# Three early query and key loads in the raw words' ring, a later third sequence, and block (0, 2) ahead of group 1

## The chip, the core and the metric

The kernel runs on one core of one Trainium2 chip. The metric is the device time of one execution in microseconds (us); three runs of the kernel before gave 728.9, 729.03 and 730.33, median 729.03.

## The reference

Three layers follow one another, all in float32.

```python
def _attn_ref(q, k, v):                      # (4, 8, 576, 64)
    scores = scale * np.matmul(q, k.transpose(0, 1, 3, 2))
    mask_local = (rel >= 0) & (rel < stride)             # heads 0 to 3, stride 32
    mask_strided = (rel >= 0) & (pos[None, :] % stride == pos[:, None] % stride)   # heads 4 to 7
    ...
    return np.matmul(attn, v)                # softmax of the masked scores times v

def _moe_ref(x, w_in, w_out, s, b):          # x (2304, 512), w_in (512, 2048), w_out (2048, 512)
    r = np.maximum(x @ w_in, 0.0)
    return (s * (r * r) + b) @ w_out

def _moe2_ref(x, w_gate, w1, w2):            # 8 experts, 288 tokens each, routed by the order of the logits
    ...
        h = np.maximum(x[mask] @ w1[e], 0.0)
        out[mask] = h @ w2[e]
```

The inputs of the second layer come as float64 words ("raw words"); the kernel makes float32 of them on the chip.

## The kernel before

**Stages.** `run` calls `mix1`, which holds the attention and the first product of the second layer; then come the second product with the routing, and the eight experts. Only `mix1` is touched. A matmul in full precision is three matmuls: every operand is split into a high part (`xh`, `wh`, `u`) and the rest (`xl`, `wl`).

**Attention.** Four sequences b of 576 tokens. `attention` yields its units, a head pair hp and a half hf each: `attn_pair` for the strided pairs, `attn_unit` for the local ones. A unit loads queries and keys (`load_unit`, L222: a tile `qk`), makes scores on PE (L264 mask, L271 products), takes the maximum on DVE (L289, L390), the exponential on ACT (L314, L395), scales on DVE, transposes on PE (L329, L420), copies to `eT` on ACT (L335, L432), multiplies with v on PE (L341, L443), and copies to `xb` on ACT (L363, L448). For the sequences 2 and 3 the mask is added on DVE instead (L307). Two pipes tick through the units: `att` for the sequences 0 and 1, `att2` for 2 and 3. `LOADLAG`, `lag` and the `yield`s say how many ticks lie between the steps of a unit.

**Words.** `prep` turns the raw words of `w_in` into `win[fc]`, fc = 0 to 15: load (L514), ACT L539, four DVE operations (L542 to L548), then `split` (ACT L524 for `wh`, DVE L526 for `wl`).

**Groups.** The tokens are cut into six groups g of 384. `group_x` (L480) splits a group's columns into `xh` (ACT L493) and `xl` (DVE L496). `h_step(g, fc)` (L633) is one block: twelve matmuls of 384 columns on PE (L641; xh times wh, xl times wh, xh times wl), two ACT operations (L653, L654), and a store to `ud` (L657). In what follows h(g, fc) is such a block.

**Order.** The program's order is each engine's order: the schedule is written by hand (`manual_schedule`). A first loop of `mix1` counts k and ticks `att`, from k = `A2K` on also `att2`, until 14 units are done; at k = 33 and 37 (`H0`) it issues h(0, 0) and h(0, 1), at k = 34 eight matmuls that only keep PE busy (L469). A second loop then walks through `seq`: after the first two blocks (1, 0), (1, 1), (0, 2), (1, 2), (0, 3), (1, 3), (2, 0), (2, 1) and so on, one block for each pass, with a tick of the pipes ahead of it. The subtractions of group 0 are collected in `self.subs` and issued at k = 30 (`XL`); those of later groups at once.

**Rings.** A tile comes from a ring of buffers, and a load into it waits until what used the buffer before is through. `qk` has the ring "u" of four (`UB`), so the load of unit n waits for the scores of unit n - 4. `wide` has the ring "rw" of four (`RW`), which before the experts holds the raw words of `w_in` alone. PE's results go to eight banks (`ps`). All loads of this stage are issued by SP, in order; a load that waits holds back those behind it.

Of the kernel before, what the change touches and what calls it, by code (L numbers as in the profile page):

```python
# [8 lines left out]
F32 = mybir.dt.float32  # L9
# [20 lines left out]
def _f(ap):  # L30
    return ap.bitcast(F32)
# [14 lines left out]
class Pipe:  # L46


    def __init__(self, items, every=1):
        self.items, self.every, self.t, self.live, self.started = iter(items), every, 0, [], 0  # L50
# [27 lines left out]
class Body:  # L78
# [21 lines left out]
    FP = 9  # L100
    FC = 8
    UB = 4
    WL = 64
    P1S = 31
    A2K = 35
    TM = 2
    FE = (12, 12, 4, 8)
    PS = (18, 30, 32, 36)
# [29 lines left out]
    def __init__(self, ctx, tc, a, dbg=()):  # L138
        self.tc, self.nc, self.a, self.dbg = tc, tc.nc, a, dbg
        self.c = ctx.enter_context(tc.tile_pool(name="c", bufs=1))  # L140
        self.w = ctx.enter_context(tc.tile_pool(name="w", bufs=self.WS))
        self.xf = ctx.enter_context(tc.tile_pool(name="xf", bufs=2))
        self.xs = ctx.enter_context(tc.tile_pool(name="xs", bufs=self.XS))
        self.p2 = ctx.enter_context(tc.tile_pool(name="p2", bufs=2))
        self.pp = ctx.enter_context(tc.tile_pool(name="pp", bufs=8, space=bass.MemoryType.PSUM))
        self.dr = ctx.enter_context(tc.tile_pool(name="dr", bufs=1, space=bass.MemoryType.DRAM))
        self.n = 0

    def nm(self, s):
        self.n += 1  # L150
# [71 lines left out]
    def load_unit(self, b, hp, hf):  # L222
        nc, a = self.nc, self.a
        loc = hp < 2
        w = 320 if loc and not hf else 288
        qk = self.p2.tile([128, 640], F32, tag="u", name=self.nm("qk"), bufs=self.UB)[:, :2 * w]
        if loc and not hf:
            src = a["q0"][b, hp]
        else:
            src = a["q1"][b, hp // 2 * (1 + hf), hp % 2]  # L230
        nc.sync.dma_start(qk, src.rearrange("p a t -> p (a t)"))
        return qk.rearrange("p (a t) -> p a t", a=2)
# [247 lines left out]
    def group_x(self, g, dc):  # L480
        nc = self.nc
        S, G = self.S, self.G
        if g == 2:
            h, l = (self.wt([128, G], F32R, n) for n in ("xh", "xl"))
        else:
            h, l = (self.xs.tile([128, G], F32R, tag=n, name=self.nm(n)) for n in ("xh", "xl"))
        t = g * G
        while t < (g + 1) * G:
            b = t // S
            e = min((b + 1) * S, (g + 1) * G)  # L490
            src = self.xb[b][:, dc, t - b * S:e - b * S]
            o = slice(t - g * G, e - g * G)
            nc.scalar.copy(h[:, o], src)  # L493

            def sub(l=l[:, o], h=h[:, o], src=src):
                nc.vector.tensor_tensor(l, src, _f(h), op=ALU.subtract)  # L496

            if g:
                sub()
            else:  # L500
                self.subs.append(sub)
            t = e
        self.xg.setdefault(g, {})[dc] = h, l
# [233 lines left out]
    def mix1(self):  # L737
# [24 lines left out]
        self.late = self.x2_late()  # L762
        self.late_pipe = Pipe(self.late_step(g, fc) for g in range(self.NG) for fc in range(16))
        lead = len(self.H0)
        seq = [(0, fc) for fc in range(lead)] + [(1, 0), (1, 1), (0, 2), (1, 2), (0, 3), (1, 3), (2, 0), (2, 1)]
        for fc in range(2, 14):
            seq += [(0, fc + 2), (2, fc), (1, fc + 2)]
        seq = [s for s in seq if s[1] < 16 - self.TAIL * (s[0] > 0)]
# [7 lines left out]
        while self.units < 14 or not self.win or ready:  # L776
            rest, self.rest = self.rest, []
            if k in self.H0:
                assert len(self.xg[0]) == 4 and not self.subs
                main.tick()  # L780
            self.attend(att, att2 if k >= self.A2K else None, mid=first.tick if k == self.P1A else None)
            for part in rest:
# [20 lines left out]
        while True:  # L803
            g, fc = seq[n] if n < 96 else (n // 16, n % 16)
            k += 1
            if n == 4:
                self.small_loads()
            if n >= self.P1S:
                prep1.tick()
            if len(self.win) < 16:  # L810
                prep.tick()
                if len(self.win) <= fc:
                    continue
            if n == 10:
                att2.every = self.AE
            self.attend(att, att2)
            while ready and self.units >= ready[0][0]:
                self.group_x(*ready.pop(0)[1:])
            if g == 2 and ready:
                continue  # L820
            if n >= self.FS:
                for _ in range(self.FT):
                    if folds.started < len(order) and order[folds.started][1] >= self.nwog:
                        break
                    folds.tick()
            if n >= self.WL and (n % 2 == 0 or n >= 84) and (lout.started < self.nwog or lout.started == 16):
                lout.tick()
            if n >= 95 and self.late_pipe.t < 6:
                self.late_pipe.tick()
            if n == 44 or fc == 12 and 2 < g < 5:  # L830
                need = 8 * (((n // 16 + 2) * self.G - 1) // self.S + 1)
                while self.units < need:
                    self.attend(att2)
            if n == self.RC:
                self.route_consts()
            if n >= 96:
                for _ in range(self.LF):
                    next(self.late, None)
            live = main.tick()
            if 44 <= n < 48 or fc >= 12 and 2 < g < 5:  # L840
                self.group_x(n // 16 + 1, n % 16 - 12)
            n += 1
            if not live and not folds.live and folds.started == len(order) and lout.started == 16 and not lout.live:
                break

    def late_step(self, g, fc):
# [7 lines left out]
        if last:  # L854
            u = self.p2.tile([128, 2, 320], F32R, tag="u", name=self.nm("u"), bufs=self.UB)[:, :, :nt * 128]
            u = u[:, 0], u[:, 1]
# [324 lines left out]
    def expert(self, e, X, w1, w2):  # L1181
# [3 lines left out]
        def step(fc):  # L1185
            ps = self.layer1(fc, X, w1)
            yield
            u = self.p2.tile([128, 2, 320], F32R, tag="u", name=self.nm("u2"), bufs=self.UB)
            self.relu_split(ps, u[:, 0, :288], u[:, 1, :288])
# [192 lines left out]
```

## Time and profile before

| | |
|---|---|
| median of three runs | 729.03 us (728.9 to 730.33) |
| profiled execution, its own time | 732.19 us |
| its span, first to last instruction | 730.1 us |
| PE busy with matmuls | 717.0 us, 98% of the span |
| PEld (weight loads), DVE, ACT | 643.2, 490.8, 382.6 us |
| DMA queue q1 | 129.68 MB |

The profiled execution took 732.19 us, 2.1 more than its span, and 3.2 more than the median of the runs without a profile. A row of a list in order of time has the start, the length, the engine, the line, the operation with what it writes and reads, the count, and in brackets the idle time ahead of it with what ended that. "issue" is idle time in which the engine waited for nothing that the profile shows.

### The profile page before, as it was taken

How to read it: one execution, taken by the hardware profiler on the slowest of the kernel's cores; microseconds unless marked ns; L12 is line 12 of the kernel's file. 1: busy time of each engine (PE TensorE's matmuls, PEld its weight loads, DVE VectorE, ACT ScalarE, POOL GpSimd, SP SyncE). 2: the span in 40 equal slices, each digit the busy share in tenths (PEclk: the TensorE clock that was granted, in tenths of full speed). 3: DMA queues.
4: the chain of work that ended last, by engine and by line, in shares of the span. 5: the costliest groups of instructions: out<-in, count | busy, mean ns of one | idle time of the engine just before them, and what ended most of it. 6: DMA issues, size and time to landing. Idle time of an engine off the chain costs nothing. (4 is left out here: it accounts for less than half of the span.)

```text
span 730.1 us, 16583 instructions
## 1 busy us (share of the span) xinstructions
PE 717.0 (98%) x6298; PEld 643.2 (88%) x6298; DVE 490.8 (67%) x1151; ACT 382.6 (52%) x876; POOL 58.6 (8%) x80
## 2 busy tenths in 40 slices
PE   8999999999999999999999999999999999999996
PEld 6779999999999888787888878888999999999995
DVE  6899798895653344286888888784566667667720
ACT  4788676777776565522432423241554655555521
POOL 3000000000000000000000000001212321322111
PEclk9999999999999999999999999999999999999999
DMA  8857786666988779733553424252867666765411
GB/s 235 255 164 213 234 258 197 222 204 220 317 292 274 225 250 321 251 127 121 183 163 127 160 82 132 94 163 74 275 196 234 213 177 210 238 206 158 151 33 32
DMA packets 82350, 140.16 MB, mean 192 GB/s; under 512 B 10592, under 2 KB 44128, under 8 KB 82272
## 3 DMA queue, kind: packets, MB, share of 16 engines
q1 hardware_dynamic: 79200, 129.68, 55.6%
q0 software_dynamic: 3072, 9.44, 4.2%
q8 instruction: 49, 0.80, 0.5%
q14 instruction: 29, 0.24, 0.1%
HBM read 106.32 MB, written 32.77 MB: 190 GB/s over the span
## 5 line engine op out<-in xcount | busy, mean ns | idle before, releaser
L897 PE MATMUL b<-wh,u 128*128 128x512 f32 x612 | 173.6, 388 | 0.3 <-DVE u L869 0.3
L897 PEld LDWEIGHTS b<-wh,u 128*128 128x128 f32 x612 | 110.6, 190 | 14.5 <-DVE u L869 1.3
L1197 PE MATMUL b<-u,wh 128*128 128x288 f32 x496 | 88.8, 292 | 0.0
L866 ACT CAST u<-r 128x384 fp32r<-128x384 f32 (+1 forms) x96 | 46.0, 493 | 79.2 <-DMA r<-ud 30.9
L641 PE MATMUL b<-xh,wh 128*128 128x384 f32 x384 | 83.6, 340 | 1.3 <-DVE E L307 1.2
L1172 PE MATMUL b<-X,wh 128*128 128x288 f32 x512 | 84.1, 287 | 0.1
L524 ACT CAST wh<-raw 128x512 fp32r<-128x512 f32 x128 | 73.2, 617 | 11.7 <-DVE u L869 11.7
L641 PE MATMUL b<-xh,wl 128*128 128x384 f32 x384 | 78.2, 326 | 0.0
L641 PE MATMUL b<-xl,wh 128*128 128x384 f32 x384 | 78.1, 326 | 0.0
L897 PE MATMUL b<-wl,u 128*128 128x512 f32 x204 | 77.6, 380 | 0.0
L653 ACT ACTIVATE r<-b 128x384 f32<-128x384 f32 x96 | 46.9, 489 | 57.0 <-PE b L641 51.9
L526 DVE TENSOR_TENSOR wl<-raw,wh 128x512 fp32r<-128x512 f32 x112 | 73.0, 684 | 0.4
L1197 PEld LDWEIGHTS b<-u,wh 128*128 128x128 f32 x496 | 72.9, 189 | 0.0
L1172 PEld LDWEIGHTS b<-X,wh 128*128 128x128 f32 x512 | 71.7, 189 | 1.0 <-ACT X L1139 0.3
L641 PEld LDWEIGHTS b<-xh,wh 128*128 128x128 f32 x384 | 61.8, 189 | 7.7 <-PE b L685 1.9
L641 PEld LDWEIGHTS b<-xh,wl 128*128 128x128 f32 x384 | 64.9, 189 | 0.1
L641 PEld LDWEIGHTS b<-xl,wh 128*128 128x128 f32 x384 | 64.9, 189 | 0.0
L1179 DVE SCALAR_TENSOR_TENSOR u<-b,u 128x288 fp32r<-128x288 f32 x64 | 29.1, 455 | 49.6 <-ACT u L1178 47.0
L869 DVE TENSOR_TENSOR u<-r,u 128x384 fp32r<-128x384 f32 (+1 forms) x96 | 47.8, 528 | 10.0 <-ACT u L866 10.0
L654 ACT ACTIVATE r<-r 128x384 f32<-128x384 f32 x96 | 50.5, 526 | 3.0
L1178 ACT ACTIVATE u<-b 128x288 fp32r<-128x288 f32 x64 | 26.3, 411 | 47.3 <-PE b L1172 44.9
L1197 PE MATMUL b<-u,wl 128*128 128x288 f32 x176 | 50.3, 286 | 0.0
(234 smaller groups left out, 1118.7 us busy)
## 6 DMA issues: line engine op xcount, KB each, us to landing
raw<-in_moe_w_dram SPq DMA_DIRECT2D x128, 256.0 KB
r<-ud SPq DMA_DIRECT2D x160, 192.0 KB
ud<-r SPq DMA_DIRECT2D x96, 192.0 KB
raw<-in_words_dram SPq DMA_DIRECT2D x16, 512.0 KB
raw<-in_words_dram SPq DMA_DIRECT2D x32, 256.0 KB
qk<-in_q_dram SPq DMA_DIRECT2D x24, 288.0 KB
x2d<-E SPq DMA_DIRECT2D x18, 256.0 KB
wod<-K SPq DMA_DIRECT2D x16, 256.0 KB
```

The lines of the kernel that those rows point to most:

```text
L524: nc.scalar.copy(h, W)
L526: nc.vector.tensor_tensor(l, W, _f(h), op=ALU.subtract)
L641: nc.tensor.matmul(ps[:, :self.G], w[:, dc * 128:(dc + 1) * 128], _alt(self.xg[g][dc][x]), start=(w is wh and x == dc == 0), stop=(w is wl ...
L653: nc.scalar.activation(_two(r), _nat(ps[:, :self.G]), AF.Relu)
L654: nc.scalar.activation(r, r, AF.Square)
L866: nc.scalar.copy(d[0], src)
L869: nc.vector.tensor_tensor(d[1], src, _f(d[0]), op=ALU.subtract)
L897: self.nc.tensor.matmul(**args)
L1172: self.nc.tensor.matmul(ps[:, :288], w1[dc, fh][wi][:, fs:fs + 128], _alt(X[:, xi, dc, :]), start=(k == 0), stop=(k == 11))
L1178: self.nc.scalar.activation(_two(h), _nat(ps[:, :288]), AF.Relu)
L1179: self.nc.vector.scalar_tensor_tensor(_two(l), _nat(ps[:, :288]), 0.0, _two(_f(h)), op0=ALU.max, op1=ALU.subtract)
L1197: nc.tensor.matmul(y[dc][:, :288], w[:, sl], _alt(u[:, j, :288]), start=(fc == 0 and i == 0), stop=(fc == 7 and i == 2))
```

## The change

Four edits. `WQ` names the 6th, 10th and 14th load of queries and keys (counted from 0: 5, 9, 13); these take a buffer of the ring "rw" instead of one of "u". `A2K` goes from 35 to 38, so that `att2` begins three passes later. In `seq`, (0, 2) stands ahead of (1, 0) and (1, 1). The subtraction for the last columns of group 1, `group_x(1, 1)`, is collected in `self.subs`, and the second loop issues what is collected there ahead of its tick of the pipes.

```diff
+    WQ = (5, 9, 13)
...
-    A2K = 35
+    A2K = 38
...
-        self.n = 0
+        self.n = self.nq = 0
...
-        qk = self.p2.tile([128, 640], F32, tag="u", name=self.nm("qk"), bufs=self.UB)[:, :2 * w]
+        if self.nq in self.WQ:
+            qk = self.wide([128, 1024], F32, "qk")
+        else:
+            qk = self.p2.tile([128, 640], F32, tag="u", name=self.nm("qk"), bufs=self.UB)
+        self.nq += 1
+        qk = qk[:, :2 * w]
...
-            if g:
+            if g and (g, dc) != (1, 1):
                 sub()
             else:
                 self.subs.append(sub)
...
-        seq = [(0, fc) for fc in range(lead)] + [(1, 0), (1, 1), (0, 2), (1, 2), (0, 3), (1, 3), (2, 0), (2, 1)]
+        seq = [(0, fc) for fc in range(lead)] + [(0, 2), (1, 0), (1, 1), (1, 2), (0, 3), (1, 3), (2, 0), (2, 1)]
...
                 if len(self.win) <= fc:
                     continue
+            for sub in self.subs:
+                sub()
+            self.subs.clear()
             if n == 10:
                 att2.every = self.AE
```

SP, about 13 to 20 us into the span, before (`qk` are queries and keys, `v` values, `raw` raw words; in brackets what the load waits for, PE being the scores that free its buffer):

```order
L231 DMA qk_470<-in_q_dram 128x576 [waits DMAHW4_49,PE_49]
L243 DMA v_480<-in_v_dram 96x512 [waits DMAHW5_49]
L231 DMA qk_500<-in_q_dram 128x576 [waits DMAHW6_49,PE_49]
L514 DMA raw_520<-in_words_dram 128x1024 [waits DMAHW7_49]
L243 DMA v_540<-in_v_dram 96x512 [waits DMAHW0_49]
L231 DMA qk_592<-in_q_dram 128x640 [waits DMAHW1_49,PE_49]
L231 DMA qk_635<-in_q_dram 128x576 [waits DMAHW2_49,PE_49]
```

The same place in the changed kernel:

```order
L237 DMA qk_470<-in_q_dram 128x576 [waits DMAHW4_49,PE_49]
L249 DMA v_480<-in_v_dram 96x512 [waits DMAHW5_49]
L237 DMA qk_500<-in_q_dram 128x576 [waits DMAHW6_49]
L520 DMA raw_520<-in_words_dram 128x1024 [waits DMAHW7_49]
L249 DMA v_540<-in_v_dram 96x512 [waits DMAHW0_49]
L237 DMA qk_592<-in_q_dram 128x640 [waits DMAHW1_49,PE_49]
L237 DMA qk_635<-in_q_dram 128x576 [waits DMAHW2_49,PE_49]
```

No load has moved; the tenth, qk_500, has lost its wait for PE, and the others wait for scores that are one to three units older.

PE, about 51 to 56 us, where group 1 begins, before (b are PE's banks; xh_956 is of group 1, wh_700 of win[0], qk_1111 of sequence 2):

```order
L443 MATMUL b_1130<-eT_1099,v_945 64x64 x2
L641 MATMUL b_1154<-xh_956,wh_700 128x384
L641 MATMUL b_1154<-xh_1119,wh_700 128x384
L641 MATMUL b_1154<-xh_883,wh_700 128x384
L641 MATMUL b_1154<-xh_1080,wh_700 128x384
L641 MATMUL b_1154<-xl_957,wh_700 128x384
L641 MATMUL b_1154<-xl_1120,wh_700 128x384
```

The same place in the changed kernel (xh_760 and xl_761 are of group 0, wh_1088 of win[2], qk_1082 of sequence 2):

```order
L449 MATMUL b_1109<-eT_1079,v_945 64x64 x2
L277 MATMUL b_1122<-qk_1082 36x36 x16
L647 MATMUL b_1150<-xh_760,wh_1088 128x384
L647 MATMUL b_1150<-xh_763,wh_1088 128x384
L647 MATMUL b_1150<-xh_766,wh_1088 128x384
L647 MATMUL b_1150<-xh_769,wh_1088 128x384
L647 MATMUL b_1150<-xl_761,wh_1088 128x384
```

The first scores of sequence 2 stand here now, and no longer in the middle of h(0, 1); h(0, 2) follows them in the place of h(1, 0).

DVE, about 51 to 55 us, before:

```order
L496 TENSOR_TENSOR xl_1081<-xb_369,xh_1080 128x192
L496 TENSOR_TENSOR xl_1081<-xb_872,xh_1080 128x192
L307 TENSOR_TENSOR E_103<-b_1057,mstr 36x8x36 x2
L496 TENSOR_TENSOR xl_1120<-xb_369,xh_1119 128x192
L496 TENSOR_TENSOR xl_1120<-xb_872,xh_1119 128x192
L526 TENSOR_TENSOR wl_1108<-K_983,wh_1107 128x512
```

And in the changed kernel:

```order
L502 TENSOR_TENSOR xl_1061<-xb_369,xh_1060 128x192
L502 TENSOR_TENSOR xl_1061<-xb_872,xh_1060 128x192
L532 TENSOR_TENSOR wl_1089<-K_983,wh_1088 128x512
L502 TENSOR_TENSOR xl_1099<-xb_369,xh_1098 128x192
L502 TENSOR_TENSOR xl_1099<-xb_872,xh_1098 128x192
```

The two mask additions of sequence 2 have left this place, and `wl` of win[2] goes ahead of the subtraction of `group_x(1, 1)`.

## Rows read from the trace of the kernel before

**Rows 1.** The page: busy time; DMA queues (packets, MB, share); issues (count, KB)

```profile
PE 717.0 (98%) x6298; PEld 643.2 (88%) x6298; DVE 490.8 (67%) x1151; ACT 382.6 (52%) x876; POOL 58.6 (8%) x80
...
q8 instruction: 49, 0.80, 0.5%
...
raw<-in_words_dram SPq DMA_DIRECT2D x16, 512.0 KB
```

**Rows 2.** What PE waited for, whole span: us in total, times, longest

```profile
PE b L264 <- DVE identb L189: 3.2, 1, 3.2
PE b L271 <- issue: 1.5, 1, 1.5
PE b L641 <- DVE E L307: 1.2, 1, 1.2
PE b L897 <- DVE u L869: 0.3, 1, 0.3
```

**Rows 3.** Busy time of each engine by stretch, granted clock (PEclk), DMA share

```profile
16.00:20.00 4.00, 4.00 (x92) 3.24 (x91) 3.67 (x10) 3.21 (x17) 0.00 (x0) 1.00 0.71 191
21.20:24.50 3.30, 3.27 (x131) 2.78 (x131) 2.52 (x7) 3.30 (x15) 0.00 (x0) 1.00 1.03 291
...
28.00:31.40 3.40, 3.40 (x40) 2.78 (x36) 3.15 (x7) 1.32 (x6) 0.00 (x0) 0.50 0.90 288
...
60.00:100.00 40.00, 40.00 (x424) 37.73 (x424) 34.97 (x63) 28.44 (x58) 0.00 (x0) 1.00 0.79 250
```

**Rows 4.** PE in order of time, around the early stall

```profile
15.03 1.04 PE L271 MATMUL b<-qk 64*64 64x96 f32 x20
...
23.79 0.68 PE L271 MATMUL b<-qk 64*36 64x36 f32 x28
25.97 0.26 PE L271 MATMUL b<-qk 64*36 64x36 f32 x4 [1.50 <-issue]
...
27.78 1.73 PE L271 MATMUL b<-qk 64*64 64x96 f32 x20
```

**Rows 5.** DMA queues from 23.0 to 23.5 us: packets, MB, share

```profile
q8 instruction: 1, 0.02, 16.2%
```

**Rows 6.** Who waited for whom, 0 to 75 us: SP's loads, PE's weight loads

```profile
PEld b L271 <- DMA qk<-in_q_dram: 0.4, 2, 0.3
...
SPq L231 <- PE b L271: 8.3, 8, 1.9
```

**Rows 7.** PE in order of time, from h(0, 1) to h(0, 3)

```profile
46.35 0.92 PE L641 MATMUL b<-xh,wh 128*128 128x384 f32 x4
47.10 0.81 PE L641 MATMUL b<-xl,wh 128*128 128x384 f32 x4
47.84 0.75 PE L271 MATMUL b<-qk 64*36 64x36 f32 x32
48.53 0.75 PE L420 MATMUL b<-identf,E 128*96 128x128 f32 x4
49.21 0.80 PE L443 MATMUL b<-eT,v 96*64 96x64 f32 x20
49.94 0.92 PE L641 MATMUL b<-xh,wl 128*128 128x384 f32 x4
50.69 0.60 PE L420 MATMUL b<-identf,E 128*96 128x128 f32 x4
51.22 0.69 PE L443 MATMUL b<-eT,v 96*64 96x64 f32 x16
53.15 0.92 PE L641 MATMUL b<-xh,wh 128*128 128x384 f32 x4 [1.24 <-DVE E L307]
...
62.74 0.81 PE L641 MATMUL b<-xh,wh 128*128 128x384 f32 x4
```

**Rows 8.** ACT in order of time, the same stretch

```profile
48.23 0.72 ACT L432 COPY eT<-b 96x384 f32<-96x384 f32 x2
...
50.33 0.66 ACT L432 COPY eT<-b 96x256 f32<-96x256 f32 x2
51.75 0.62 ACT L524 CAST wh<-K 128x512 fp32r<-128x512 f32 x1 [0.77 <-DVE K L548]
```

**Rows 9.** DVE in order of time, the same stretch

```profile
52.18 0.92 DVE L307 TENSOR_TENSOR E<-b,mstr 36x288 f32<-36x288 f32 x2
...
61.32 0.69 DVE L526 TENSOR_TENSOR wl<-K,wh 128x512 fp32r<-128x512 f32 x1
```

## The prediction

> **What bounds the kernel now.** I read the page's busy times first: PE is busy for 717.0 us of a span of 730.1, 98%, more than any other engine [rows 1]. So an edit is worth what it takes off PE's idle time or adds to it, and anything else only if it makes PE's own work longer. Next I read what PE waited for. There are three waits of more than a microsecond: 3.2 us at the start, for a constant; 1.5 us ahead of scores, for nothing that the profile shows ("issue"); and 1.2 us ahead of a block, for DVE's L307 [rows 2]. The table by stretch shows a fourth loss: from 28.0 to 31.4 us the granted clock is 0.50, that is 1.2 GHz and not 2.4 [rows 3]. Behind 53 us PE has no idle time worth a row until the second product; from 60 to 100 us it is busy for 40.00 of 40.00 us [rows 3]. The four edits all act ahead of about 150 us, so they can win at most the second and third wait and the slow stretch. What they can lose is a new wait.
>
> **The change part by part. Removed: the wait at 51.9 us.** PE's h(1, 0) starts at 53.15 after 1.24 us of idle time, which DVE's L307 ended [rows 7]. L307 is the mask addition of sequence 2 and runs from 52.18 to 53.10 [rows 9]; it reads a bank that PE wants back. With A2K at 38 the scores that L307 reads are made later, and L307 leaves this place in DVE's order; h(0, 2), which now comes first, needs group 0, long split, and win[2]. So that wait goes. What is late next is found by replaying PE from 46.35 with the durations of the rows, start to start. The first eight matmuls of h(0, 1) end at 47.84. The scores that stood there (0.69 us) are gone, so the transposes run from 47.84 to 48.52 (0.68). The products behind them want eT, which ACT finishes at 48.23 + 0.72 = 48.95 [rows 8]: a new wait of 0.43. They take 0.73, the last four matmuls of h(0, 1) take 0.75, the transposes 0.53 [rows 7]: 50.96. The next products want eT at 50.33 + 0.66 = 50.99 [rows 8]: 0.03 of waiting. They take 0.69: 51.68. The first scores of sequence 2, moved here, take 0.69: 52.37. The wh of win[2] is ready at 51.75 + 0.62 = 52.37 [rows 8]. So h(0, 2) starts at 52.37 with the same work behind it as h(1, 0) had at 53.15: **0.78 us won**. Of the 1.24 us, 0.46 come back as waits for eT, because the moved scores had covered ACT. Bounds: nothing, if some other operand binds at 53.1; the whole 1.24 if ACT, too, runs ahead.
>
> **Moved: blocks, subtraction, sequence 2.** The order of the blocks costs nothing on PE, since the same twelve matmuls are issued; what counts is that operands are there. The wl of win[2] is the next DVE operation behind wh: 52.37 + 0.69 = 53.06, and the last four matmuls of h(0, 2) want it 1.5 us after 52.37 (46.35 to 47.84, [rows 7]), at 53.86. The deferred subtraction of group_x(1, 1) stands behind that, 0.63 us long, done by about 53.7; h(1, 0) starts two microseconds after 52.37, and wants it later still. Win[3], for h(0, 3), gains: DVE's wl for it ends at 61.32 + 0.69 in the kernel before, behind a mask addition, a maximum and a subtraction of sequence 2, and these now come later; PE starts h(0, 3) at 62.74 [rows 7, 9]. Sequence 2 itself starts three passes later, and the orders of both kernels are the same again from group 3 on. In between DVE has to do the same work in less time: from 60 to 100 us it is busy for 34.97 of 40 us [rows 3], and what is pushed in there is about 4 us of mask additions, maximum, sum and scaling of one pair. That fits, but not by much. I put the cost at nothing, covered by the matmuls of the blocks; if that cover is gone, one wait like the present one, 1.24 us, is the price.
>
> **Added and removed waits on SP.** Three loads no longer wait for a buffer of "u", and the loads behind them wait for older scores. SP's waits of this kind add up to 8.3 us in eight waits [rows 6]; most go. All that waited for these loads are two of PE's weight loads, 0.4 us together, and PE's matmuls have no idle time there [rows 2, 6]; so the data are early already and the direct gain is nil. In "rw" the raw words lose buffers: the fourth raw load now waits for the first raw words' last DVE operation, the fifth for scores of the fourteenth load. Both have happened when SP comes to them, and nobody waited for raw words. The indirect effect is what I can't price from one row. The stall of 1.50 us at 24.5 falls inside the scores of one unit: 28 matmuls run, then nothing, then the last four [rows 4]. All share one tile, so it is not data. An instruction packet moved at 23.0 to 23.5 us [rows 5], while the DMA engines were at 1.03 of their time [rows 3], with PE issuing 131 matmuls in 3.3 us, 40 a microsecond, against 23 from 16 to 20 us. I read it as instructions that came late because their packet stood among loads. The change issues loads earlier: it fills the stretch of 16 to 20 us, where the DMA share is 0.71 [rows 3], and then, with buffers free, SP can push more into 20 to 26 us. The first shortens the queue at 21 us, the second keeps it full. I take zero, since PE's own order up to here is the same, and the DMA share around 21 to 24 us stays near its limit either way. Bounds: the stall and the slow stretch behind it go, or there is one more of each. The slow stretch costs, start to start, 1.66 us for scores of 64x96 that took 0.97 at 15.03 [rows 4], a ratio of 1.7; over 3.4 us that is 3.4 - 3.4 / 1.7 = 1.4. So the bounds are -2.9 and +2.9 us.
>
> The Trainium skill, in "Runtime: NRT & Kernel Launch", section "Instruction fetch mechanics", says that an engine's instructions are fetched in blocks of 16 KiB ahead of use and that crossing a block is mostly hidden. By that rule the loads could not matter to PE, and only the 0.78 would be left; the trace's 1.50 us without a waited-for operand does not look hidden, but no run here shows yet that it is the fetch. In "DMA: Bandwidth & Descriptors", section "Queues, rings and completion order", the skill says that a DMA engine takes turns between queues, packet by packet. By that a deeper queue of loads would not hold an instruction packet longer, which speaks against the slower rival below; the trace cannot tell.
>
> **The sum.** The profiled execution took 732.19 us; its span is 730.1, and 2.1 lie around it. With 0.78 less the span is 729.3. Carried to the median of the runs, 729.03, which is 3.2 below the profiled time: 729.03 - 0.78 = **728.2 us**, 0.1% less.
>
> **The rivals.** *The early stall shrinks or goes.* For it: loads are spread more evenly ahead of 20 us. Against it: the densest stretch of PE stays as it is. Time: 728.2 - 1.5 = 726.7 for the stall alone, 728.2 - 2.9 = 725.3 with the slow stretch. *The early stall grows, the slower case.* Place: PE's instructions between 21 and 26 us. SP, no longer held back, has queries, values and 512 KB of raw words [rows 1] in the queue when the packet is asked for. Each 0.1 us that it lands later is 0.1 us on PE; from 0.78 us on the change is a loss, and with one more stall of 1.5 and another slow stretch of 1.4 the time is 728.2 + 2.9 = 731.1. For it: the DMA share is at 1.03 already. Against it: the total of bytes is the same. *The gain is given back* by a PE wait between 60 and 150 us, where sequence 2 is now squeezed: 728.2 + 0.8 to 1.2, about 729.2. For it: DVE at 34.97 of 40 us; against it: PE waits for nothing there now. *The change doesn't do what it says* where h(0, 2) finds its bank held by another eviction, ACT's, until about 53.1: 729.0. DVE's order shows L307 gone, so I count this with the last.
>
> **How the numbers follow.** Forecast 728.2 with 0.50, the stall shrinks 0.22 (725.3 to 726.7), the stall grows 0.13 (729.5 to 731.1), given back 0.15 (729.0 to 729.4). What a measurement of this kernel can tell from no change is about 0.2%, 1.5 us: faster means below 727.6, slower above 730.5. The forecast's own range is 727.5 to 728.9. Faster takes the shrinking stall, 0.22, and 0.07 of the forecast's edge: 0.29. Slower takes the upper half of the growing stall and a little of the unforeseen: 0.11. Same is 0.60. The range of 8 in 10 runs from 725.4, near the full gain of the stall, to 730.2, the middle of the growing stall.
>
> **What would show it.** In the changed kernel's profile, PE's row for h(0, 2) should start near 52.4 us with no wait for L307, and a short wait for ACT's eT should stand near 48.5. The row "issue" for PE tells the rivals apart: 1.5 us as now, or less, or more, and so does the granted clock from 20 to 35 us. Any new wait of PE between 60 and 150 us, above all for DVE, would say that the gain was given back. The prediction is wrong if the early stall moves by more than a microsecond, or if h(0, 2) waits for something that I held to be early.

## The result and the profile after

The changed kernel takes 732.62 us (median of 12 runs, 730.91 to 738.22); the kernel before took 729.96 beside it (12 runs, 728.43 to 730.63). The ratio, which compares means, is 1.0056 [1.0036, 1.0075]: **slower by 0.56%, 4.1 us**; the medians lie 2.7 us apart, for a few long executions pull the mean up. The prediction, 728.2 us and at most 730.2, was wrong in direction too. Single executions now lie 7.3 us apart, before 2.2. The profiled execution took 737.56 us (span 735.8), one of the longest; the kernel before had 732.19 (730.1).

The page of the changed kernel, busy time and the queue q8 (it answers to [rows 1]):

```profile
PE 720.9 (98%) x6298; PEld 646.3 (88%) x6298; DVE 490.6 (67%) x1151; ACT 383.7 (52%) x876; POOL 58.3 (8%) x80
...
q8 instruction: 50, 0.82, 0.5%
```

What its PE waited for (it answers to [rows 2]):

```profile
PE b L270 <- DVE identb L190: 3.2, 1, 3.2
PE b L449 <- ACT eT L438: 1.9, 1, 1.9
PE b L277 <- issue: 1.9, 2, 1.6
PE b L347 <- ACT eT L341: 0.5, 1, 0.5
PE b L906 <- DVE u L878: 0.3, 1, 0.3
```

The wait for L307 is gone; two waits for ACT's eT are new; "issue" has grown from one stall to two. The table by stretch of the changed kernel (columns as in [rows 3]):

```profile
16.00:20.00 4.00, 4.00 (x95) 3.31 (x94) 2.86 (x6) 2.68 (x15) 0.00 (x0) 1.00 1.00 292
...
24.50:28.00 3.50, 1.91 (x41) 1.51 (x37) 1.16 (x3) 1.82 (x4) 0.00 (x0) 0.80 0.93 245
28.00:31.40 3.40, 3.40 (x41) 2.60 (x41) 2.46 (x5) 1.65 (x4) 0.00 (x0) 0.50 0.85 298
31.40:35.00 3.60, 3.60 (x73) 2.75 (x71) 2.76 (x6) 2.24 (x13) 0.00 (x0) 0.72 0.60 186
...
164.40:166.50 2.10, 0.17 (x3) 0.09 (x4) 0.91 (x3) 2.10 (x6) 0.00 (x0) 1.00 0.71 206
166.50:170.00 3.50, 3.50 (x29) 3.35 (x30) 2.29 (x7) 3.42 (x9) 0.00 (x0) 0.51 0.34 129
```

The DMA share from 16 to 20 us is 1.00 instead of 0.71 [rows 3]. The half clock (1.2 of 2.4 GHz) lasts 1.4 us in the row of 0.80 ((1 - 0.80) / 0.5 x 3.5), 3.4 in the row of 0.50 and 2.0 in that of 0.72: 6.8 us instead of 3.4. A second such stretch follows at 166.5 us, behind an idle time of 1.94 us. PE of the changed kernel, in order of time, at the early stall and at the late one:

```profile
7.66 1.86 PE L277 MATMUL b<-qk 64*64 64x96 f32 x20
...
24.72 0.68 PE L277 MATMUL b<-qk 64*36 64x36 f32 x28
26.99 0.34 PE L277 MATMUL b<-qk 64*36 64x36 f32 x4 [1.59 <-issue]
...
155.94 0.77 PE L347 MATMUL b<-eT,v 36*64 36x36 f32 x32 [0.49 <-ACT eT L341]
...
163.67 0.81 PE L647 MATMUL b<-xh,wl 128*128 128x384 f32 x4
166.42 1.25 PE L449 MATMUL b<-eT,v 96*64 96x64 f32 x20 [1.94 <-ACT eT L438]
```

The stall stands at the same instructions as in [rows 4], behind 28 scores of one unit and ahead of its last four. The two profiled executions differ by 5.7 us of span. Late waits: 0.49 + 1.94 = 2.4; the late slow stretch, at the ratio of 1.7 of the prediction, 3.4 - 3.4 / 1.7 = 1.4; the longer early slow stretch 1.4; more "issue" 0.4; scores at 7.66 us that took 1.86 us instead of 1.04, ahead of anything the change touches and with the granted clock at 1.00 in both profiles, 0.8, for a reason that stays open; less L307's 1.24. That makes 5.2.

### The profile page after: what moved, and what is told of

Its sections match the earlier page's. It is cut to its first block, busy times and chain, and to the rows that moved or that the text cites. A ratio compares the mean times of both kernels' runs of the same rounds, so it can differ in the third digit from the quotient of the medians.

```text
span 735.8 us, 16584 instructions
## 1 busy us (share of the span) xinstructions
PE 720.9 (98%) x6298; PEld 646.3 (88%) x6298; DVE 490.6 (67%) x1151; ACT 383.7 (52%) x876; POOL 58.3 (8%) x80
```

## The experiments

Two theories stood at first: "early" (the loads in the raw words' ring make PE's stalls longer) and "late" (the later third sequence makes PE wait for eT). Diffs are against the changed kernel, if nothing else is said; "before" runs on the same chip beside each kernel. All twelve are told.

### Each part undone

```diff
-    A2K = 38
+    A2K = 35
```

> The changed kernel with A2K back at 35; the two other parts stay. Theory 'late' (the third sequence, begun later, makes one load of values wait 7.3 us on SP from 139.7 us on, so stores of r come late, ACT waits for a buffer, PE waits 0.5 and 1.9 us for eT at 155 and 164 us and then runs at a lower clock): SP's load of the 96x128 values waits 0.4 us instead of 7.3, PE has no wait for eT behind 150 us, and the time is 0.999 to 1.001 of before. Theory 'early' (the three loads in the raw words' ring lengthen the stretch of clock 0.5 around 30 us from 3.4 to 6.8 us): the stretch stays at about 6.8 us and the time at 1.003 to 1.006.

Measured: 732.03 us (729.13 to 734.65, 12 runs), 1.0026 [1.0009, 1.0042]. No wait for eT behind 150 us, as "late" has it, but the time is not that of before: it is close under the 1.003 of "early". Each theory has a part of the loss. PE of this kernel stalled three times:

```profile
25.90 0.26 PE L277 MATMUL b<-qk 64*36 64x36 f32 x4 [1.06 <-issue]
...
32.34 0.64 PE L277 MATMUL b<-qk 64*36 64x36 f32 x26 [0.40 <-issue]
...
39.03 1.54 PE L277 MATMUL b<-qk 64*64 64x96 f32 x15 [1.81 <-issue]
```

Between these stalls, by stretch (PE's and PEld's counts are the first two in brackets):

```profile
25.85:32.30 6.45, 6.04 (x125) 4.67 (x125) 5.85 (x12) 4.21 (x17) 0.00 (x0) 1.00 0.88 289
32.30:39.00 6.70, 4.87 (x126) 3.94 (x125) 6.00 (x14) 6.23 (x23) 0.00 (x0) 1.00 1.05 264
```

The stalls are 250 and 251 instructions of PE apart. The page counts 6298 + 6298 such instructions and 49 packets on q8, about 257 for each, so the stalls may well stand where one packet's instructions end and the next one's begin. The times of the packets bear it out. In the thirteen traces that have an "issue" wait (all but the one with six stores on POOL) there are 19 such waits, of 0.2 to 2.1 us; each ends 1.3 to 1.7 us after a packet of q8 has landed, and for the wait ahead of the four scores that landing lies anywhere between 23.1 and 25.3 us. So PE waits for that packet.

```diff
-    WQ = (5, 9, 13)
+    WQ = ()
```

> The changed kernel with all loads of queries and keys in their own ring again; the later start of sequence 3's pipe and the order of the blocks stay. Theory 'late': time 1.003 to 1.008 of before, the 7.3 us wait of SP and PE's 1.9 us wait for eT near 164 us are there. Theory 'early': the stretch of clock 0.5 is 3.4 us again and the time is 0.998 to 1.001.

Measured: 731.09 us (729.91 to 734.4), 1.0024 [1.0012, 1.0036], between the ranges of the two theories. What its PE waited for:

```profile
PE b L449 <- ACT eT L438: 1.5, 2, 1.2
PE b L347 <- ACT eT L341: 0.5, 1, 0.5
...
PE b L277 <- issue: 0.2, 1, 0.2
```

The early stall is 0.21 us and no stretch of half clock follows; the late waits are there, 0.49 and 1.22. Against the changed kernel the three loads cost 1.0056 - 1.0024, 0.32% or 2.3 us, by the two intervals give or take 1.6.

```diff
-            if g and (g, dc) != (1, 1):
+            if g:
...
-        seq = [(0, fc) for fc in range(lead)] + [(0, 2), (1, 0), (1, 1), (1, 2), (0, 3), (1, 3), (2, 0), (2, 1)]
+        seq = [(0, fc) for fc in range(lead)] + [(1, 0), (1, 1), (0, 2), (1, 2), (0, 3), (1, 3), (2, 0), (2, 1)]
```

> The changed kernel with (1, 0), (1, 1) ahead of (0, 2) again and the subtraction of group_x(1, 1) issued at once. Both theories expect the time of the changed kernel, 1.003 to 1.008 of before, since neither the late wait nor the early stretch hangs on it. My step on the block order: L307 has left its place through A2K alone, so h(1, 0) now waits for its own xl instead, and PE loses 0.3 to 0.8 us near 52 us against the changed kernel.

Measured: 735.01 us (731.32 to 738.97, 6 runs), 1.0084 [1.0054, 1.0115], a little above the forecast; its interval overlaps the changed kernel's. L307 has left its place, and h(1, 0) waited 0.50 us near 50 us, as much as the step on the block order said, but for ACT's xh and not for its own xl. The rest of the loss is not told apart with six executions.

### One part alone

Only the three loads, against the kernel before:

```diff
+    WQ = (5, 9, 13)
...
+        if self.nq in self.WQ:
+            qk = self.wide([128, 1024], F32, "qk")
...
```

> The kernel before with one part of the change alone: three loads of queries and keys in the raw words' ring. Theory 'packets' (loads that are let go earlier fill the DMA queues from 14 us on, PE's instruction packets wait behind them, and PE stops at the same instructions in every kernel, the last four scores of one unit, until its packet has landed): the stall there is 0.7 to 1.8 us, single executions differ by several us, time 1.001 to 1.005 of before; PE's wait for L307 near 52 us (1.24 us in the kernel before) is still there; no wait for eT behind 150 us. Rival 'order' (the spread comes from the blocks' order or the later sequence): 0.999 to 1.0005 and no more spread than before.

Measured: 731.53 us (729.12 to 737.11), 1.0027 [1.0005, 1.0049]. The spread comes with this part. In the profiled execution the stall stood one place on, ahead of the 15 scores at 37.98 us, and was 2.09 us long. I had expected L307's wait to stay; it was gone: L307 ended at 52.46 us, and PE came to h(1, 0) at 53.14 only. Early stalls and that wait hide each other in part.

Only the order of blocks and the late subtraction:

```diff
-            if g:
+            if g and (g, dc) != (1, 1):
...
-        seq = [(0, fc) for fc in range(lead)] + [(1, 0), (1, 1), (0, 2), (1, 2), (0, 3), (1, 3), (2, 0), (2, 1)]
+        seq = [(0, fc) for fc in range(lead)] + [(0, 2), (1, 0), (1, 1), (1, 2), (0, 3), (1, 3), (2, 0), (2, 1)]
...
+            for sub in self.subs:
+                sub()
+            self.subs.clear()
```

> The kernel before with the new order of blocks and the late subtraction alone. My step of 0.78 us: the wait for L307 near 52 us goes, waits of 0.1 to 0.5 us for eT near 46 us take part of its place, and with neither the three loads nor the later sequence there is nothing to lose: 0.998 to 1.000 of before. Rival: L307 only moves and another wait takes its place, 0.9995 to 1.001.

Measured: 729.96 us (729.21 to 730.79), 0.9998 [0.9989, 1.0007]. The time fits both; the trace decides for the rival:

```profile
51.78 0.89 PE L647 MATMUL b<-xh,wh 128*128 128x384 f32 x4 [1.35 <-ACT xh L499]
```

The wait has only changed its cause. The whole gain near 52 us needs both the order and the later sequence; with the later sequence and the old order, above, 0.50 us of waiting were left.

### What makes eT late

One load issued by POOL (`hp` 1 of sequence 3, the 96x128 values):

```diff
-            nc.sync.dma_start(t.rearrange("p h d -> p (h d)"), a["v0"][b, hp])
+            (nc.gpsimd if (b, hp) == (3, 1) else nc.sync).dma_start(t.rearrange("p h d -> p (h d)"), a["v0"][b, hp])
```

> The changed kernel, with one load (the 96x128 values of sequence 3, second head pair, the one that held SP for 7.3 us) issued by POOL instead of SP; it still waits for its buffer, but nothing stands behind it. Theory 'late': the store of r that waited behind it goes at about 142 us instead of 147.4, ACT's wait of 2.95 us for a buffer of r and PE's wait of 1.9 us near 164 go, and the time is 0.999 to 1.002 of before. Theory 'early': nothing changes, 1.003 to 1.008.

Measured: 732.09 us (730.22 to 734.09, 8 runs), 1.0035 [1.0021, 1.0049]. Waits for eT of 0.49 and 1.13 us stay: that load's hold on SP is not the cause.

Six stores of r by POOL:

```diff
+    UP = range(33, 39)
...
-        nc.sync.dma_start(self.ud[g][fc], r)
+        (nc.gpsimd if self.nu in self.UP else nc.sync).dma_start(self.ud[g][fc], r)
+        self.nu += 1
```

> The changed kernel, with six stores of r (between 137 and 162 us) issued by POOL, where nothing holds them back, instead of SP, where they stand behind a store of wod that waits for DVE. Theory 'stores' (ACT waits 2 to 3 us for the store that frees the buffer of its next r, and eT, behind it on ACT, comes late): ACT's wait for a store goes, PE's wait for eT of 1.1 to 1.9 us near 161 us goes or falls under 0.4, the one of 0.49 near 151 stays; 1.1 to 1.9 us less than the changed kernel, 1.001 to 1.004 of before. Rival (ACT is late through DVE or PE anyway): the wait of 1.1 to 1.9 stays and the time is the changed kernel's, 1.003 to 1.008.

Measured: 731.77 us (729.96 to 736.78), 1.0035 [1.0018, 1.0052]. The wait of 0.49 went, that of 1.2 stayed, against my expectation. ACT of this kernel, in order of time:

```profile
157.10 1.19 ACT L370 COPY xb<-b 128x288 f32<-128x288 f32 x2
160.10 0.47 ACT L439 COPY eT<-b 96x384 f32<-96x384 f32 x1 [1.80 <-DMA ud<-r]
```

Now eT itself waits for a store of r. In the changed kernel r waited (here its ACT):

```profile
163.32 0.49 ACT L659 ACTIVATE r<-b 128x384 f32<-128x384 f32 x1 [2.95 <-DMA ud<-r]
163.84 0.52 ACT L660 ACTIVATE r<-r 128x384 f32<-128x384 f32 x1
164.27 0.74 ACT L545 ACTIVATE K<-raw 128x256 f32<-128x256 f32 x2
164.91 1.14 ACT L369 COPY xb<-b 128x288 f32<-128x288 f32 x2
165.84 0.52 ACT L438 COPY eT<-b 96x384 f32<-96x384 f32 x1
```

and SP issued the stores late, behind the store of wod, which waits for DVE's K, and behind two loads (SP, in order of time):

```profile
152.37 0.42 SPq L663 DMA_DIRECT2D ud<-r  x1
157.62 0.33 SPq L561 DMA_DIRECT2D wod<-K  x1
158.00 1.20 SPq L520 DMA_DIRECT2D raw<-in_words_dram  x2
159.30 0.38 SPq L663 DMA_DIRECT2D ud<-r  x1
```

So the new theory is "buffers": the ring of 60 small tiles (`w`) runs so short here that a tile ACT wants to write gets the buffer of an r whose store has just been issued. Test: give twelve r other buffers, without the three loads (`WQ = ()`).

```diff
-    WQ = (5, 9, 13)
+    WQ = ()
...
+    RR = range(33, 45)
...
-        r = self.wt([128, self.G], F32, "r")
+        if self.nr in self.RR:
+            r = self.wide([128, 1024], F32, "r")[:, :self.G]
+        else:
+            r = self.wt([128, self.G], F32, "r")
+        self.nr += 1
```

> The changed kernel without the three loads in the raw words' ring, and with twelve tiles r (from about 133 us on) in that ring, which holds no raw words any more by then: the ring of 60 small buffers has four more free. Theory 'buffers' (with the later third sequence, a tile that ACT writes near 158 us takes the buffer of an r whose store is still under way, and PE gets its eT late): ACT's wait for a store near 158 us goes, PE's wait of 1.2 us for eT near 161 goes or falls under 0.3, the one of 0.49 us near 151 may stay; 1.2 to 1.7 us less than the same kernel without this (1.0024), so 0.9995 to 1.001 of before. Rival 'ACT is late anyway' (as with the stores on POOL): the wait of 1.2 us stays, 1.002 to 1.003.

Measured: 729.08 us (728.44 to 730.71), **0.999 [0.9981, 0.9999]**. What its PE waited for:

```profile
PE b L271 <- DVE identb L191: 3.2, 1, 3.2
PE b L278 <- issue: 0.4, 1, 0.4
PE b L911 <- DVE u L883: 0.3, 1, 0.3
PE b L450 <- ACT eT L439: 0.3, 1, 0.3
PE b L648 <- ACT wh L531: 0.2, 1, 0.2
```

Both late waits of PE are gone. ACT still waits for a store, but half as long as the 2.06 us of the same kernel with r in the small ring, and PE no longer feels it:

```profile
159.39 0.49 ACT L664 ACTIVATE r<-b 128x384 f32<-128x384 f32 x1 [1.06 <-DMA ud<-r]
```

Against that kernel the gain is 1.0024 - 0.999, 0.34% or 2.5 us, give or take 1.1. It is the one version here whose interval lies under 1, though its mean is only 0.1% under. Taking twelve tiles out of the ring frees buffers and also changes which buffer each later tile gets; which of the two did it is not told apart here.

`A2K` = 37, no loads in "rw":

```diff
-    WQ = (5, 9, 13)
+    WQ = ()
...
-    A2K = 38
+    A2K = 37
```

> The kernel before with the new order of blocks and A2K = 37; no loads in the raw words' ring. The tiles of the words and of sequence 3 take other buffers than with 38. If the loss behind 150 us is a matter of which buffer comes round, and not of sequence 3 being late as such, the waits for eT at 151 and 161 us go: with the waits for L307 and xh near 52 us gone too, 0.998 to 0.9995 of before. Rival 'late as such': two passes later still costs about what three cost, 1.001 to 1.002.

Measured: 730.0 us (729.02 to 730.96), 1.0001 [0.9992, 1.001]. No wait behind 150 us: two passes later does not cost what three cost, so lateness as such is not it. The gain I expected did not come: PE waits 0.90 us at 72.4 for DVE's scaling of E (L326), in the stretch in which sequence 2 is squeezed.

### What makes PE's instructions late

Three loads fewer, then eight (with `A2K` = 35 and a longer `SK`). `WQ` stands as in the changed kernel, but the 10th load is left out in both and the 14th in the second, so of the three early loads two remain in the first and one in the second:

```diff
+    SK = (8, 9, 11)
...
+        if self.nq in self.SK:
+            qk = self.lastqk
...
-        nc.sync.dma_start(qk, src.rearrange("p a t -> p (a t)"))
+        if new:
+            nc.sync.dma_start(qk, src.rearrange("p a t -> p (a t)"))
```

> The changed kernel without three of its loads of queries and keys (the 9th, 10th and 12th; the units take the tile of the unit before, so their attention is another one): 0.86 MB less between 13 and 20 us, PE's instructions are the same. Theory 'packets': the instruction packet that came at 24.0 us comes at 22.5 or earlier, the stall in the scores (1.59 us in the changed kernel) falls under 0.3, and single executions agree better; time 1.000 to 1.003 of before. Rival 'density' (PE runs out of instructions there because it issues 40 matmuls in a microsecond, whatever the loads): the stall stays at 0.7 to 1.6 us.

Measured: 734.68 us (732.42 to 737.71, 6 runs), 1.0065 [1.0045, 1.0086]; stalls of 1.23 and 0.41 us, and late in the trace a wait of 2.82 us for eT with a stretch of half clock behind it.

> The changed kernel with A2K back at 35 and with eight loads of queries and keys left out (the 9th, 10th and 12th to 17th; the units take an earlier tile, so their attention is another one): about 2.4 MB less between 13 and 35 us. It was 1.0026 of before with all loads, with 729 to 735 us for single executions. Theory 'packets': with the DMA share under 0.9 from 20 to 36 us the stalls at the scores (1.06, 0.40 and 1.81 us with all loads) fall under 0.3 each, executions agree within 2 us, and the time falls to 0.996 to 0.999 of before. Rival 'density' (PE outruns its instruction supply there, whatever the loads): stalls of 0.7 us and more stay, and the spread of 5 us with them.

Measured: 730.63 us (729.88 to 732.89), 1.0013 [1.0002, 1.0023]; stalls of 1.23 and 0.40 us. By the signs on record both speak for "density": the first stall stayed, and the times lie above the ranges of "packets". But the queues did not get emptier, so neither tells the theories apart: SP, with nothing to wait for, sent later loads sooner, and the DMA share from 18 to 20 us was 0.95 and 1.04, with all loads 0.98 in the changed kernel. Only with eight loads out did the third stall and half of the spread go. The opposite is cleaner: add traffic to the fastest kernel, the one with twelve r in "rw", and change nothing else (diff against that kernel):

```diff
+    XT = {1: (0, 1), 2: (2, 3, 4), 3: (5, 6, 7)}
...
+        for i in self.XT.get(self.nv, ()):
+            nc.gpsimd.dma_start(self.ud[5][i][:96], t.rearrange("p c h d -> p (c h d)")[:, :384])
+        self.nv += 1
```

> The fastest kernel so far (later third sequence, new order of blocks, twelve r in the raw words' ring, no loads of queries and keys there: 0.999 of before, stall at the scores 0.40 us), with eight extra copies of 0.15 MB each from tiles of values to scratch memory in DRAM, issued by POOL from about 14 to 21 us. PE's instructions and what it waits for stay the same. Theory 'packets' (an instruction packet comes late when the DMA engines are full between 16 and 23 us): the DMA share from 16 to 20 us rises from 0.6 to 0.8 to about 1.0, the third packet starts a microsecond or more later than at 22.2 us, the stalls add up to 1.0 to 3 us, single executions differ by 4 us and more, and the time is 1.001 to 1.004 of before. Rival 'density' (PE outruns its supply by itself) or 'WQ does it by some other way than the traffic': stalls of 0.2 to 0.6 us and 0.998 to 1.000 of before.

Measured: 731.55 us (729.66 to 734.88), 1.0022 [1.0007, 1.0037], against 0.999 without the copies. By stretch, first without them and then with them:

```profile
16.00:20.00 4.00, 4.00 (x93) 3.24 (x91) 3.69 (x10) 3.22 (x17) 0.00 (x0) 1.00 0.70 179
...
28.00:32.00 4.00, 4.00 (x109) 3.33 (x108) 3.83 (x10) 3.41 (x16) 0.00 (x0) 1.00 0.90 293
```

```profile
16.00:20.00 4.00, 4.00 (x92) 3.12 (x90) 3.79 (x10) 3.50 (x19) 1.28 (x3) 1.00 1.01 273
...
28.00:32.00 4.00, 4.00 (x71) 3.20 (x69) 3.56 (x7) 1.72 (x10) 0.00 (x0) 0.66 0.99 346
```

And PE's wait, the only one of its kind in either, first without and then with the copies:

```profile
24.86 0.26 PE L278 MATMUL b<-qk 64*36 64x36 f32 x4 [0.40 <-issue]
```

```profile
25.68 0.26 PE L282 MATMUL b<-qk 64*36 64x36 f32 x4 [1.50 <-issue]
```

The third instruction packet began at 23.18 us instead of 22.23 and landed at 24.19 instead of 23.35; PE went on 1.5 us later in both. The stall rose from 0.40 to 1.50 us, and the half clock came back behind it. PE's instructions and operands are the same, and the two intervals of the time do not overlap. Traffic alone does it: "packets" holds.

## Why the prediction was wrong

**The wait for L307: right.** I had 0.78 us. In the kernel with r in "rw", which has this part and neither loss, 0.28 for eT stands near 46 us in place of my 0.43 and 0.03, and 0.20 for wh ahead of h(0, 1), which PE reaches earlier there: 0.76 won. From the start of h(0, 1) to that of h(0, 2) it takes 6.00 us, in my replay 6.02. The median is 0.75 under the 729.83 of before beside it, but the interval allows 0.1 to 1.4, so that the time agrees so well is in part luck.

**The early stall, "I take zero": the step that failed first.** I named the mechanism (an instruction packet among loads) and then left its size as it was, since the stretch of 21 to 24 us was full already. But the loads filled the stretch ahead of it: from 16 to 20 us the share went from 0.71 to 1.00, and where copies alone made it rise so, from 0.70 to 1.01, the third packet began 0.95 us later. With the loads in "rw", or with the copies, the stalls of the nine profiled executions add up to 0 to 3.3 us, 1.6 in the mean (1.9, 3.3, 0.7, 1.5, 2.1, 0, 1.6, 1.6, 1.5); in the four other kernels that have neither, 0.2 to 0.4, and in that of before 1.5. Early stretches of half clock stand in four of the nine (6.8, 6.8, 3.4 and 3.4 us), in the mean 2.3 us, which at the ratio of 1.7 cost 0.9; in the four others there is none. That is 2.5 us against 0.3, and the price in the times is 2.3 us in the mean. A single trace can show the opposite: the profiled execution of before stalled for 1.50 us at a share of 0.71, and the one with six stores on POOL, at 1.01, did not stall at all; its third packet landed at 23.26 us, and PE came to those four scores only at about 25.2. So the share from 16 to 20 us does not settle the stall of one execution. The rival "the stall grows" was this, with 2.9 us as its price; I gave it 0.13. My sign for being wrong, the early stall moved by more than a microsecond, did not show it: between the two profiles PE's "issue" grew by 0.4 us only, since the one of before had a long stall already. On SP my reading was off too: its waits of queries and keys for scores fell from 8.3 to 6.0 us only, and a load of raw words, which I held free to go, waited 3.0 us for scores.

The Trainium skill, in "Runtime: NRT & Kernel Launch", section "Instruction fetch mechanics", has the crossing of a block mostly hidden. The traces disagree for this stretch: the wait for one packet cost PE up to 2.09 us with the three loads, and adding copies alone took it from 0.40 to 1.50. By that rule the loads would have cost next to nothing; they cost 2.3 us. "DMA: Bandwidth & Descriptors", section "Queues, rings and completion order", has a DMA engine take turns between queues, packet by packet. Here 1.2 MB of foreign copies put the instruction packet back by 0.95 us; they went on a queue of their own (q0), so this shows a delay by more traffic and does not test whether a deeper queue of loads (q1) delays it.

**The base was misread too.** The profiled execution of before stood 3.2 us over the median, and I took that for a cost that all executions share. The four other kernels whose early loads are those of before stalled 0.2 to 0.4 us there and had no slow stretch; the profiled one had 1.50 us and 3.4 us at half clock, 1.5 + 1.4 = 2.9 together. That the 3.2 us are this stall is argued from those four traces, not shown for the runs without a trace; but of the 112 executions of the kernel before that were timed beside the others only four took more than 732 us, so such a loss is rare in them. If it is this stall, the lower end of my range, 725.4, took a loss away that the median hardly has.

**Sequence 2 later, "I put the cost at nothing": the step that failed second.** I took the four edits to act ahead of about 150 us and looked for the price on DVE from 60 us on; with `A2K` = 38 PE waits for nothing from there to 150 us. The price came at 151 to 165 us and through a resource that I had not counted, the ring of small buffers: 0.49 + 1.22 us of waits without the three loads, 0.49 + 1.94 and a slow stretch in the changed kernel's profile, 2.5 us in the mean. My rival had 1.24 us as its price, in the wrong place and with the wrong mechanism. For `A2K` = 37 alone the squeeze showed, with 0.90 us.

**The sum.** -0.7 + 2.5 + 2.3 = 4.1 us, the measured 0.56%. That the three meet it says nothing: they are the steps from before to the kernel with r in "rw", from there to the one without the three loads, and from there to the changed one, so they must add up to it. What checks them are other pairs. The loads cost 1.0026 - 0.9998, 0.28%, between the kernel with the new order alone and the one with `A2K` = 35, and 0.27% alone on the kernel before, 2.0 us each. The later sequence costs 1.0056 - 1.0026, 0.30% or 2.2 us, with the loads and 1.0024 - 0.9998, 0.26% or 1.9 us, without them, its gain near 52 us taken off already. With intervals of 0.1 to 0.2% on each ratio these agree.

## What to carry to other kernels

A load that is let go earlier is not free because its data were early already: if it fills a gap in the DMA queues, other things that come by DMA, the engine's own instructions among them, can come later. A change in the program's order changes which buffer of a shared ring each tile gets; print what each tile waits for far behind the edit as well, and look for a writer on a busy engine that waits for a store just issued. A single profiled execution that stands above the median of the runs is to be searched for a loss of its own before it serves as the base of a sum.

## What the runs showed of the hardware

- PE's stalls without an operand to wait for stood at the same few instructions in thirteen of the fourteen traces (in the one with three of them 250 and 251 instructions of PE apart), and lasted 0.2 to 2.1 us. All 19 ended 1.3 to 1.7 us after a packet of the instruction queue (q8) had landed.
- Copies of 1.2 MB on another queue, with PE's instructions unchanged, put such a packet back by 0.95 us and cost 0.32% (0.999 to 1.0022).
- PE's granted clock was 0.50 for 3.4 or 6.8 us behind idle times of 1.50 (twice), 1.59, 1.81, 1.94, 2.09 and 2.82 us, and stayed at 1.00 behind 1.06, 1.13, 1.22, 1.23, 1.31 and 1.35. At the ratio of 1.7 a stretch of 3.4 us costs 1.4 us on top of the idle time.
- Two losses in a row did not add up: with a stall of 2.09 us at 36 us, the wait for L307 at 52 us was gone.
